# An attention and MLP kernel on one core: where the weights are converted, where GpSimd forms x0, and when pair 1 is loaded

## The chip, the cores and the metric

One core of a Trainium2 chip runs the whole kernel. The metric is the device time of one execution in microseconds (us). Engines: PE is TensorE (matmuls), DVE is VectorE, ACT is ScalarE, POOL is GpSimd, and SP is SyncE, which here only issues DMAs. Each engine runs its own queue in order.

## The reference

```
scores = q k^T / 8 + bias          # 4 batches, 8 heads, 576 x 576, head size 64
bias   = relu(psi(i,j) w1 + b1) w2 # a small MLP over positions, the same for all batches
attn   = exp(scores - max) / (sum + 1e-9)
x      = attn v                    # reshaped to 2304 tokens x 512
h      = x w_in                    # 512 -> 2048
out    = (h tanh(softplus(h))) w_out   # 2048 -> 512
```

`w_in` and `w_out` are float64 in DRAM; everything else is float32. The kernel splits each matmul operand into a high part (fp32r) and the remainder (low), and adds high x high, high x low and low x high.

## The kernel before

Three phases follow each other in one hand-ordered program (no planner reorders it; the order in which the Python issues instructions is the order of each engine's queue).

*Bias phase.* 36 groups (`idx` 0 to 35) of 16 positions each: `make_h` forms four `ht` tiles on ACT or DVE, PE multiplies them by w2 into `bps`, `evac` scales the result on ACT into one of eight `bt` buffers, and SP stores it to `bias_d` in DRAM. At the indices in `BIAS_AT` SP loads finished bias rows back for the first head pair. At `SOFT_AT` the first three attention steps are already issued. In between, `load_raw(1)` (SP: q/k rows and v of pair 1), `load_hi(1)` (a DMA from POOL's queue) and `load_weights` (SP: two weight tiles of 512 KB) are issued at fixed indices.

*Attention.* 16 pairs (a batch and two heads), 5 steps each, 80 steps (`NS`). A step does `scores` on PE, `add_bias` with the maximum on DVE, `exps` on ACT, `transposes` on PE and ACT of the step two before, and `pv_duo` on PE. For the next pair POOL subtracts the high from the full operand: `split_k` at a pair's second step, `split_q` at its third (for pair 1 both are issued at step 3). One MLP weight tile is converted over four steps: `high` (float64's upper word, scaled), `low` (a shift), two merging instructions on DVE (L125, L127), then ACT copies the high part and POOL subtracts the low part (L138). Half of the 32 tiles are done here. Near the end x of the first token block is loaded (`load_x`), with the reciprocals of the sums (`load_r`, two halves into one buffer), and POOL multiplies them (L375) at steps NS-8 and NS-4.

*MLP.* 72 units. A unit is one chunk of 128 hidden features for a block of 512 tokens (or two chunks for the block of 256). `hidden` is 12 matmuls, followed by Exp on ACT and two instructions on DVE (L600, L601). `gate`, one unit later, is Ln and Exp on ACT, two products on DVE (L611, L612), `ghi` on ACT and `glo = e - ghi` (L614, on POOL up to unit 23, then on DVE). `project`, three units later, is 12 matmuls. The first halves of blocks 0 and 1 (units 0 to 15) come first, then their second halves; `split_x(1)` prepares block 1 during units 2 to 7, and after block 0's first half its sums are copied out (L639). `convert` does the other 16 weight tiles: once before the loop's units, then behind the gate at units 3, 5, 7 and from 8 on at three of four units, with `high` on ACT and the subtraction on POOL.

The change touches `conv_weights` (L107 to L130), `ahead` and `split` (L358 to L391), the calls at L534 to L539 with `BIAS_AT` (L468), `gate` (L604) and the MLP loop (L698 to L743).

Of the kernel before, what the change touches and what calls it, by code (L numbers as in the profile page):

```python
# [7 lines left out]
F32 = mybir.dt.float32  # L8
F32R = mybir.dt.float32r
U32 = mybir.dt.uint32  # L10
AF = mybir.ActivationFunctionType
ALU = mybir.AluOpType
# [7 lines left out]
P = 128  # L20
# [26 lines left out]
def kernel(ctx: ExitStack, tc, qk, v, wb, w2, w_in, w_out, psia, psi4, rinv, eye, out):  # L47
# [18 lines left out]
    convp = sbuf("conv", 2)  # L66
# [19 lines left out]
    EARLY, HALF = 4, len(order) // 2  # L86
    ring = sbuf("ring").ring((HALF - EARLY) * 4096 + 2560)
    w_hi, w_lo = {}, {}
    todo, w64, w32 = list(order), [], []

    def alloc_weights(jobs, p):
        for job in jobs:
# [3 lines left out]
    def load_weights():  # L96
        while todo and len(w64) < 2:
            kind, g, k = job = todo.pop(0)
            w = convp.tile([P, 512, 2], U32, name="w64")
            if kind == "i":  # L100
                src = w_in[k * P:(k + 1) * P, g * 512:(g + 1) * 512]
            else:
                src = w_out[(4 * g + k) * P:(4 * g + k + 1) * P, :]
            sp.dma_start(out=w.rearrange("p f t -> p (f t)"), in_=src.bitcast(U32))
            w64.append((job, w))

    def conv_weights(on_act):  # L107

        job, w = w64.pop(0)
        c = convp.tile([P, 512], F32, name="w32")
        cu = c.bitcast(U32)
        high = convp.tile([P, 512], F32, name="high", bufs=1)
        low = convp.tile([P, 512], U32, name="low", bufs=1)
        hu = high.bitcast(U32)
        if on_act:
            act.mul(high, w.bitcast(F32)[:, :, 1], 2.0 ** -112)  # L118
        else:
            dve.tensor_scalar(high, w.bitcast(F32)[:, :, 1], 2.0 ** -112, None, op0=ALU.mult)  # L120

        def parts():
            dve.tensor_scalar(low, w[:, :, 0], 29, None, op0=ALU.logical_shift_right)
            yield False
            dve.scalar_tensor_tensor(cu, hu, 3, low, op0=ALU.logical_shift_left, op1=ALU.bitwise_or)  # L125
            yield False
            dve.scalar_tensor_tensor(cu, hu, 0x80000000, cu, op0=ALU.bitwise_and, op1=ALU.bitwise_or)  # L127
            w32.append((job, c))
            yield True
        return parts()  # L130

    def split_weights(eng):
        job, c = w32.pop(0)
        if job not in w_hi:
            w_hi[job] = ring.tile([P, 512], F32R, name="wh{}{}{}".format(*job))
            w_lo[job] = ring.tile([P, 512], F32R, name="wl{}{}{}".format(*job))
        act.copy(w_hi[job], c)
        eng.tensor_tensor(w_lo[job], c, w_hi[job].bitcast(F32), op=ALU.subtract)  # L138
# [188 lines left out]
            sp.dma_start(out=x_d[b][:, hp, 512:576], in_=x[:, 0:64])  # L327

    LAG = 2
    conv = []  # L330
    alloc_weights(order[:EARLY], wpool)

    x_raw, x_r, x_hi, x_lo = {}, {}, {}, {}
# [9 lines left out]
    def load_r(blk, r, h0, h1):  # L343

        t0, n = blocks[blk]
        for off, m, b, s in _x_runs(t0, n):
            while m:
# [7 lines left out]
                                 in_=src.unsqueeze(0).to_broadcast([64, h1 - h0, k]))  # L355
                off, m, s = off + k, m - k, s + k

    def ahead(n):  # L358

        i, x = divmod(n, 5)  # L360
        if x == 4 and i + 2 < NPAIR:
            load_hi(i + 2)
            load_raw(i + 2)
        if i % B == B - 1 and i // B + 1 < HP:
            load_bias(i // B + 1, ORDER[x])
        if n == NS - 11:
            load_x(0, x0)
        if n in (NS - 10, NS - 6):
            x_r[0] = x0.tile([P, 2, TB], F32, name="xr", bufs=1)
            h0 = 0 if n == NS - 10 else 2  # L370
            load_r(0, x_r[0], h0, h0 + 2)
        if n in (NS - 8, NS - 4):
            h0 = 0 if n == NS - 8 else 2
            for d in range(2):
                pool.tensor_tensor(x_raw[0][:, h0 + d], x_raw[0][:, h0 + d], x_r[0][:, d], op=ALU.mult)  # L375

    def split(n):

        i, x = divmod(n, 5)
        if (x == 1 or n == 3) and i + 1 < NPAIR:  # L380
            split_k(i + 1)
        if (x == 2 or n == 3) and i + 1 < NPAIR:
            split_q(i + 1)

        for _ in range((1, 1, 1, 1, 1)[x]):
            if not conv and w64[0][0] in order[:HALF]:
                conv.append(conv_weights(x == 2))
            elif conv and next(conv[0]):
                conv.clear()
                load_weights()  # L390
                split_weights(pool)  # L391

    def step(n):
        i, x = divmod(n, 5)
# [70 lines left out]
    spent = {"v": 0.0, "a": 0.0}  # L465
    maker = {}
    SOFT_AT = (18, 27, 35)
    BIAS_AT = (12, 20, 24, 32, 36)  # L468
    for idx, t in enumerate(ts):
        spent["a"] += 1.0 + (1.9 if idx in SOFT_AT else 0.0)  # L470
        spent["v"] += (1.7 if idx in SOFT_AT else 0.0) + (1.4 if idx in (9, 12) else 0.0)
# [37 lines left out]
    for idx in range(NB + 2):  # L509
        if idx < NB:  # L510
            t = ts[idx]
            make_h(idx + 2)
            n = reach(t)[2]
            ps = bps.tile([P, 1024], F32, name="bps")
            for a in range(0, n, 512):
                for cg in range(4):
                    pe.matmul(ps[cg * 32:cg * 32 + 32, a:min(a + 512, n)], w2t,  # L517
                              h_t[idx, cg][:, a:min(a + 512, n)], start=True, stop=True)
            bps_t[t] = ps
        if 1 <= idx <= NB:  # L520
            evac(ts[idx - 1])
        if idx == 1:
            load_raw(0)
        if idx == 9:
            split_k(0)
        if idx == 12:
            split_q(0)
        if idx in BIAS_AT:
            load_bias(0, ORDER[BIAS_AT.index(idx)])
        for lag, do in enumerate((scores, add_bias, exps)):  # L530
            if idx - lag in SOFT_AT:
                for u in range(2 if lag == 2 else 1):
                    do(SOFT_AT.index(idx - lag), *((u,) if lag == 2 else ()))
        if idx == 14:  # L534
            load_raw(1)
        if idx == 18:
            load_hi(1)
        if idx == 26:
            load_weights()  # L539
    bias_scope.close()  # L540

# [16 lines left out]
    def split_x(blk, parts):  # L558
        n = blocks[blk][1]
        if blk not in x_hi:  # L560
            x_hi[blk] = xp.tile([P, HP, TB], F32R, name="xhi")
            x_lo[blk] = xp.tile([P, HP, TB], F32R, name="xlo")
        for x, d in parts:
            raw, hi, lo = (y[blk][:, d, :n] for y in (x_raw, x_hi, x_lo))
            if x == "h":
                if blk:

                    dve.tensor_tensor(raw, raw, lo.bitcast(F32), op=ALU.mult)
                act.copy(hi, raw)  # L569
            else:  # L570
                dve.tensor_tensor(lo, raw, hi.bitcast(F32), op=ALU.subtract)  # L571
# [29 lines left out]
        dve.scalar_tensor_tensor(e, e, 2.0, e, op0=ALU.add, op1=ALU.mult)  # L601
        h_t[blk, fs] = (h, e)

    def gate(blk, fs, eng=dve):  # L604
        r = mp.tile([P, TB], F32, name="r")
        ghi = mp.tile([P, TB], F32R, name="ghi")
        glo = mp.tile([P, TB], F32R, name="glo")
        h, e = h_t.pop((blk, fs))
        act.activation(r, e, AF.Ln, bias=two[:, 0:1])
        act.activation(r, r, AF.Exp, scale=-1.0)  # L610
        dve.tensor_tensor(e, h, e, op=ALU.mult)  # L611
        dve.tensor_tensor(e, e, r, op=ALU.mult)  # L612
        act.copy(ghi, e)  # L613
        eng.tensor_tensor(glo, e, ghi.bitcast(F32), op=ALU.subtract)  # L614
        gs[blk, fs] = (ghi, glo)

    def stage(name):
# [77 lines left out]
    wq = sbuf("wq")  # L695
    y_ps = psum("y_ps", 1)
    alloc_weights(order[HALF:], wq)
    done = []  # L698

    def convert():  # L700

        if done:
            split_weights(done.pop())
        if w64:
            for _ in conv_weights(True):
                pass
            load_weights()
            done.append(pool)

    gate(*units[0], pool)  # L710
    hidden(*units[1])
    convert()
    gate(*units[1], pool)
    hidden(*units[2])

    for k in range(2, len(units) + LAG2):
        if k < len(units):
            blk, fs = units[k]
            f = fs[0]
            if k < FH:  # L720
                split_x(1, XPARTS[:2] if k == 2 else XPARTS[2:4] if k == 3 else XPARTS[k:k + 1])
            elif blk == 1 and f == FH:
                fetch_x(2)
            elif blk == 0:
                if f == FH:
                    fetch_r(2)
                if f == FH + 5:
                    load_kept()
                if f >= FH + 3:
                    split_x(2, {3: XPARTS[:2], 4: XPARTS[2:4]}.get(f - FH, XPARTS[f - FH - 1:f - FH + (f == NFC - 1)]))  # L730
            elif 2 <= blk < len(blocks) - 1:
                if f == 2:
                    fetch(blk + 1)
                if f >= 8:
                    split_x(blk + 1, XPARTS[f - 8:f - 8 + len(fs)])
            if k > 2:
                hidden(blk, fs)
        if k >= LAG2:
            project(*units[k - LAG2])
        if 2 <= k - 1 < len(units):  # L740
            gate(*units[k - 1], pool if k < 3 * FH else dve)
        if k > 2 and (k % 4 < 3 if k >= FH else k % 2):
            convert()  # L743


# [55 lines left out]
```

## Time and profile before

| | us |
|---|---|
| median of 3 runs | 753.96 (752.93 to 755.56) |
| the profiled execution | 754.99 |
| its span in the profile | 752.1 |

| engine | busy us in the span |
|---|---|
| PE | 712.2 |
| DVE | 514.3 |
| ACT | 467.9 |
| POOL | 181.8 |

In the trace the bias phase and the first steps fill the time to about 66 us, attention lasts to about 328, and the MLP the rest. Matmuls are pipelined, so a busy PE is not a PE at full rate: compare how much work passes in a stretch. A row of a timeline has the start, the us of the whole entry and its instruction; the brackets hold the idle time before it and what ended that. A row of busy time by stretch has the stretch and its length, the busy us and instructions of PE, PEld, DVE, ACT and POOL, PE's granted clock (1.00 is full), the DMA engines' share and GB/s. A row of groups by line has the count, busy us, mean ns, and the idle time before.

### The profile page before, as it was taken

What the parts mean: (1) busy time and instruction counts of PE and PEld (TensorE: products, weight loads), DVE (VectorE), ACT (ScalarE), POOL (GpSimd) and SP (SyncE); (2) the same over time, 40 slices, a digit from 0 to 9 for tenths busy, and PEclk for the clock granted to TensorE, in tenths of its full rate; (3) what the DMA queues carried; (4) which work ended last, traced back from release to release, by engine and by line L of the source; (5) the groups of instructions that cost most, each with busy time, mean ns of one, the idle gap of its engine ahead of it and who ended that gap; (6) DMA issues with size and microseconds to landing.
All of it is one profiled execution on the core that took longest, in us unless ns stands there. A gap on an engine that the chain in (4) does not pass through costs nothing.

```text
span 752.1 us, 11589 instructions
## 1 busy us (share of the span) xinstructions
PE 712.2 (95%) x4144; PEld 544.4 (72%) x4144; DVE 514.3 (68%) x987; ACT 467.9 (62%) x995; POOL 181.8 (24%) x113
## 2 busy tenths in 40 slices
PE   6769999999999999899989999999999999999997
PEld 2226777777777777658767776688998888888886
DVE  7995767768677764346877777777576666665554
ACT  6877877887888787665455455555454554444443
POOL 1110443565444453402343433300100000000000
PEclk9979999999999999999998999999999999999999
DMA  8987759648866977141113311132304000010001
GB/s 276 308 256 249 242 165 298 214 161 276 258 205 186 299 242 222 45 128 37 57 56 112 112 57 56 29 113 79 90 1 120 22 0 1 1 56 1 1 0 57
DMA packets 46681, 95.68 MB, mean 127 GB/s; under 512 B 13456, under 2 KB 22304, under 8 KB 44576
## 3 DMA queue, kind: packets, MB, share of 16 engines
q1 hardware_dynamic: 43744, 74.80, 32.9%
q0 software_dynamic: 2304, 19.92, 7.8%
q8 instruction: 32, 0.52, 0.3%
q10 hardware_dynamic: 576, 0.22, 0.1%
q14 instruction: 25, 0.20, 0.1%
HBM read 73.48 MB, written 21.45 MB: 126 GB/s over the span
## 4 chain that ended last, share of the span: by engine, by line
PE 66%; DVE 17%; ACT 8%; issue 4%; DMA 2%; POOL 2%; SPq 1%; DVEq 0%; ACTq 0%; POOLq 0%
PE y L632 18%; PE h L594 17%; PE s L220 11%; PE o L315 8%; PE tp L282 6%; DVE w L127 3%; PE bps L517 3%; DVE w L125 2%; DVE e L601 2%; DVE e L612 2%; DVE e L600 2%; PE o L319 2%; DVE e L611 2%; DMA xr<-r_d 2%; ACT high L118 1%
## 5 line engine op out<-in xcount | busy, mean ns | idle before, releaser
L251 ACT ACTIVATE pt<-pt,m 128x576 f32<-128x576 f32 x144 | 112.7, 784 | 53.0 <-DVE m L236 52.4
L236 DVE CUSTOM_DVE_ANT_0 pt<-s,bias 128x576 f32<-128x576 f32 x144 | 103.7, 752 | 55.3 <-PE s L220 53.5
L613 ACT CAST ghi<-e 128x512 fp32r<-128x512 f32 x72 | 44.7, 621 | 143.7 <-DVE e L612 139.7
L632 PE MATMUL y<-who,glo 128*128 128x512 f32 x288 | 114.4, 397 | 5.9 <-POOL glo L614 5.9
L632 PE MATMUL y<-who,ghi 128*128 128x512 f32 x288 | 114.1, 396 | 4.4 <-ACT xraw L639 2.2
L632 PE MATMUL y<-wlo,ghi 128*128 128x512 f32 x288 | 113.2, 393 | 0.0
L594 PE MATMUL h<-xhi,whi 128*128 128x512 f32 (+1 forms) x320 | 80.3, 372 | 1.0 <-ACT xhi L569 0.9
L594 PE MATMUL h<-xlo,whi 128*128 128x512 f32 (+1 forms) x320 | 79.0, 368 | 0.0
L594 PE MATMUL h<-xhi,wli 128*128 128x512 f32 (+1 forms) x320 | 78.8, 368 | 0.0
L220 PE MATMUL s<-qkhi 128*128 128x288 f32 x320 | 77.1, 322 | 0.7 <-issue 0.4
L315 PE MATMUL o<-main,vt 128*64 128x320 f32 (+1 forms) x512 | 75.8, 418 | 1.2 <-DVE x L322 1.2
L600 DVE TENSOR_SCALAR e<-e 128x512 f32<-128x512 f32 x72 | 36.5, 507 | 57.5 <-ACT e L599 57.5
L220 PEld LDWEIGHTS s<-qkhi 128*128 128x128 f32 x320 | 49.5, 189 | 34.1 <-issue 28.6
L220 PE MATMUL s<-qkhi,qlo 128*128 128x288 f32 x320 | 69.1, 297 | 3.6 <-POOL qlo L182 3.6
L177 POOL TENSOR_TENSOR qkhi<-rawqk,qkhi 64x1216 fp32r<-64x1216 f32 x15 | 42.7, 2844 | 118.5 <-DMA rawqk<-in_qk_dram 55.2
L632 PEld LDWEIGHTS y<-who,glo 128*128 128x128 f32 x288 | 54.6, 190 | 22.1 <-POOL glo L614 10.9
L599 ACT ACTIVATE e<-h 128x512 f32<-128x512 f32 x72 | 42.6, 591 | 43.5 <-PE h L594 43.5
L283 ACT COPY main<-tp 128x512 f32<-128x512 f32 x128 | 68.0, 581 | 0.7 <-PE tp L282 0.2
L632 PEld LDWEIGHTS y<-who,ghi 128*128 128x128 f32 x288 | 54.5, 189 | 19.0 <-ACT ghi L613 4.2
L282 PE MATMUL tp<-ident,pt 128*128 128x128 f32 x512 | 67.4, 275 | 0.7 <-ACT main L283 0.7
L594 PEld LDWEIGHTS h<-xhi,whi 128*128 128x128 f32 x320 | 57.8, 190 | 13.5 <-ACT xhi L569 2.4
L594 PEld LDWEIGHTS h<-xlo,whi 128*128 128x128 f32 x320 | 56.9, 189 | 10.4 <-DVE xlo L571 0.4
(75 smaller groups left out, 1210.6 us busy)
## 6 DMA issues: line engine op xcount, KB each, us to landing
qkhi<-in_qk_dram POOLq DMA_DIRECT2D x16, 1216.0 KB, 8.7
bias_d<-bt SPq DMA_DIRECT2D x36, 295.5 KB
rawqk<-in_qk_dram SPq DMA_DIRECT2D x32, 304.0 KB
w<-in_w_in_dram SPq DMA_DIRECT2D x16, 512.0 KB
w<-in_w_out_dram SPq DMA_DIRECT2D x16, 512.0 KB
vt<-in_v_dram SPq DMA_DIRECT2D x16, 320.0 KB
bias<-bias_d SPq DMA_DIRECT2D x16, 288.0 KB
out_dram<-w SPq DMA_DIRECT2D x17, 256.0 KB
```

Source lines behind the costliest of these rows:

```text
L177: (pool if i else dve).tensor_tensor(kl, qk_raw[i][64:128], kl.bitcast(F32), op=ALU.subtract)
L220: pe.matmul(s[:, j, :SH], stat[:, q0:q0 + P], hi[:, QW + kc + j * SH:QW + kc + (j + 1) * SH], start=(k == 0), stop=(k == len(todo) - 1))
L236: dve.tensor_tensor_reduce(out=halves(pt[:, sl]), in0=s[:, :, :SH], in1=halves(bt[:, sl]), scale=-0.125, scalar=BIG, op0=ALU.add, op1=ALU. ...
L251: act.activation(ps, ps, AF.Exp, bias=m[:, u:u + 1], scale=-1.0, accum_out=sums[i][:, k:k + 1])
L282: pe.transpose(tp[:, k * P:(k + 1) * P], pt[:, c0:c0 + P], ident)
L283: act.copy(main[:, h, :, off:off + P], tp.rearrange("p (k q) -> p k q", k=4))
L315: pe.matmul(o[h * 64:h * 64 + 64, :w], vt[:, h, k, :], main[:, h, k, :], start=(k == 0), stop=False, **kw)
L594: pe.matmul(h[:, u * n:(u + 1) * n], w["i", g4, d][:, r * P:(r + 1) * P], x[:, d, :n], start=(k == 0), stop=(k == 11))
L599: act.activation(e, h, AF.Exp)
L600: dve.tensor_scalar(e, e, E20, None, op0=ALU.min)
L613: act.copy(ghi, e)
L632: pe.matmul(ys[blk][t], g[:, c0:c0 + P], w, start=((blk, f) in first and k == 0), stop=((blk, f) in last and k == 2))
```

## The change

The conversion is cut into four functions with a list `half` between them: `scale_high`, `shift_low` (which also loads the next weight tile), `merge` and `sign`. In attention they keep one part per step. In the MLP a loop over all units issues, at units 0, 2, 4, 6, 7 and from 8 on at two of three, `scale_high` on ACT at the head of the unit; the other three parts stand on DVE between `ghi` and `glo` of the same unit, and `split_weights` at the head of the next, with its subtraction on DVE. `glo` is always on DVE. `split_x(1)` is spread over units 0 to 6. POOL's x0 products move one step later (NS-7 and NS-3). `load_raw(1)`, `load_hi(1)` and `load_weights` move to indices 32, 33 and 36 of the bias phase, and two entries of `BIAS_AT` change.

```diff
     todo, w64, half, w32 = list(order), [], [], []
-    def conv_weights(on_act):
+    def scale_high(eng):
         job, w = w64.pop(0)
-        c = convp.tile([P, 512], F32, name="w32")
         high = convp.tile([P, 512], F32, name="high", bufs=1)
-        low = convp.tile([P, 512], U32, name="low", bufs=1)
-        if on_act:
+        if eng is act:
             act.mul(high, w.bitcast(F32)[:, :, 1], 2.0 ** -112)
         else:
             dve.tensor_scalar(high, w.bitcast(F32)[:, :, 1], 2.0 ** -112, None, op0=ALU.mult)
+        half.append((job, w, high))
+
+    def shift_low():
+        job, w, high = half.pop(0)
+        low = convp.tile([P, 512], U32, name="low", bufs=1)
+        dve.tensor_scalar(low, w[:, :, 0], 29, None, op0=ALU.logical_shift_right)
+        half.append((job, high, low))
+        load_weights()
+
+    def merge():
+        job, high, low = half.pop(0)
+        c = convp.tile([P, 512], F32, name="w32")
+        dve.scalar_tensor_tensor(c.bitcast(U32), high.bitcast(U32), 3, low, ...)
+        half.append((job, high, c))
+
+    def sign():
+        job, high, c = half.pop(0)
+        cu = c.bitcast(U32)
+        dve.scalar_tensor_tensor(cu, high.bitcast(U32), 0x80000000, cu, ...)
+        w32.append((job, c))
...
     def ahead(n):
-        if n in (NS - 8, NS - 4):
-            h0 = 0 if n == NS - 8 else 2
+        if n in (NS - 7, NS - 3):
+            h0 = 0 if n == NS - 7 else 2
             for d in range(2):
                 pool.tensor_tensor(x_raw[0][:, h0 + d], x_raw[0][:, h0 + d], x_r[0][:, d], op=ALU.mult)
...
     def split(n):
-            if not conv and w64[0][0] in order[:HALF]:
-                conv.append(conv_weights(x == 2))
-            elif conv and next(conv[0]):
-                conv.clear()
-                load_weights()
-                split_weights(pool)
+        if half:
+            parts.pop(0)()
+        elif w64[0][0] in order[:HALF]:
+            scale_high(act if x == 2 else dve)
+            parts.extend((shift_low, merge, lambda: (sign(), split_weights(pool))))
...
-    BIAS_AT = (12, 20, 24, 32, 36)
+    BIAS_AT = (12, 20, 24, 30, 37)
...
-        if idx == 14:
+        if idx == 32:
             load_raw(1)
-        if idx == 18:
+        if idx == 33:
             load_hi(1)
-        if idx == 26:
+        if idx == NB:
             load_weights()
...
-    def gate(blk, fs, eng=dve):
+    def convert():
+        shift_low()
+        merge()
+        sign()
+
+    def gate(blk, fs):
...
         act.copy(ghi, e)
-        eng.tensor_tensor(glo, e, ghi.bitcast(F32), op=ALU.subtract)
+        if half:
+            convert()
+        dve.tensor_tensor(glo, e, ghi.bitcast(F32), op=ALU.subtract)
...
-    def convert():
-        if done:
-            split_weights(done.pop())
-        if w64:
-            for _ in conv_weights(True):
-                pass
-            load_weights()
-            done.append(pool)
-    gate(*units[0], pool)
-    hidden(*units[1])
-    convert()
-    gate(*units[1], pool)
-    hidden(*units[2])
-    for k in range(2, len(units) + LAG2):
+    SHARE = {0: XPARTS[0:1], 1: XPARTS[1:2], 2: XPARTS[2:4], 3: XPARTS[4:5], 4: XPARTS[5:6], 5: XPARTS[6:7], 6: XPARTS[7:]}
+
+    for k in range(len(units) + LAG2):
+        on = k % 3 < 2 if k >= FH else k in (0, 2, 4, 6, 7)
+        if w32:
+            split_weights(dve)
+        if on and w64:
+            scale_high(act)
         if k < len(units):
...
             if k < FH:
-                split_x(1, XPARTS[:2] if k == 2 else XPARTS[2:4] if k == 3 else XPARTS[k:k + 1])
+                split_x(1, SHARE.get(k, ()))
...
-            if k > 2:
+            if k > 0:
                 hidden(blk, fs)
         if k >= LAG2:
             project(*units[k - LAG2])
-        if 2 <= k - 1 < len(units):
-            gate(*units[k - 1], pool if k < 3 * FH else dve)
-        if k > 2 and (k % 4 < 3 if k >= FH else k % 2):
+        if 0 <= k - 1 < len(units):
+            gate(*units[k - 1])
+        elif half:
             convert()
```

## Rows read from the trace of the kernel before

**Rows 1.** The page's first part: busy us (share of the span) xinstructions

```profile
PE 712.2 (95%) x4144; PEld 544.4 (72%) x4144; DVE 514.3 (68%) x987; ACT 467.9 (62%) x995; POOL 181.8 (24%) x113
```

**Rows 2.** Chain of waits, steady MLP: start us, us, what xcount

```profile
498.92 2.72 PE h L594 x12
501.64 2.72 PE y L632 x12
```

**Rows 3.** PE in order of time, then busy time by stretch of the MLP

```profile
348.74 1.07 PE L594 MATMUL h<-xhi,whi 128*128 128x512 f32 x4
...
348.74:498.92 150.18, 139.84 (x578) 108.36 (x577) 112.97 (x157) 77.65 (x135) 53.87 (x37) 0.98 0.20 66
498.92:737.00 238.08, 238.08 (x1142) 201.00 (x1141) 151.68 (x250) 116.29 (x193) 2.59 (x2) 1.00 0.12 34
```

**Rows 4.** DVE's wait for high (total, times, longest); DVE, POOL timelines of conversions

```profile
DVE w L125 <- ACT high L118: 23.2, 15, 1.6
...
452.87 0.78 DVE L125 SCALAR_TENSOR_TENSOR w<-high,low 128x512 uint32<-128x512 uint32 x1 [1.55 <-ACT high L118]
453.69 1.67 DVE L127 SCALAR_TENSOR_TENSOR w<-high,w 128x512 uint32<-128x512 uint32 x1
...
388.07 1.75 POOL L138 TENSOR_TENSOR wli<-w,whi 128x512 fp32r<-128x512 f32 x1
```

**Rows 5.** DVE timeline at 342; DVE's groups by line, 498.92 to 737

```profile
342.65 0.42 DVE L123 TENSOR_SCALAR low<-w 128x512 uint32<-128x512 uint32 x1
...
343.90 0.69 DVE L127 SCALAR_TENSOR_TENSOR w<-high,w 128x512 uint32<-128x512 uint32 x1
...
L614 DVE TENSOR_TENSOR glo<-e,ghi 128x512 fp32r<-128x512 f32 x45 | 31.2, 692 | 33.2 <-ACT ghi L613 33.2
L612 DVE TENSOR_TENSOR e<-e,r 128x512 f32<-128x512 f32 x44 | 30.5, 693 | 4.6
...
L600 DVE TENSOR_SCALAR e<-e 128x512 f32<-128x512 f32 x44 | 18.7, 426 | 43.4 <-ACT e L599 43.4
```

**Rows 6.** PE timeline where block 0's sums are copied out

```profile
395.63 0.50 PE L632 MATMUL y<-who,ghi 128*128 128x512 f32 x1 [2.18 <-ACT xraw L639]
```

**Rows 7.** Chain of waits; PE timeline; POOL timeline, attention's last pairs

```profile
264.48 1.26 PE s L220 x8
...
281.06 1.26 PE s L220 x8
...
318.92 1.26 PE s L220 x8
...
307.43 0.85 PE L220 MATMUL s<-qkhi,qlo 128*128 128x288 f32 x2 [2.92 <-POOL qlo L182]
...
295.60 2.77 POOL L177 TENSOR_TENSOR qkhi<-rawqk,qkhi 64x1216 fp32r<-64x1216 f32 x1 [8.95 <-DMA rawqk<-in_qk_dram]
302.17 2.51 POOL L375 TENSOR_TENSOR xraw<-xraw,xr 128x512 f32<-128x512 f32 x2 [3.79 <-DMA xr<-r_d]
```

**Rows 8.** Bias phase: POOL and DVE timelines, line L490, DMA by stretch, SP

```profile
2.85 1.24 POOL L172 DMA_DIRECT2D qkhi<-in_qk_dram  x2
...
35.39 2.78 POOL L177 TENSOR_TENSOR qkhi<-rawqk,qkhi 64x1216 fp32r<-64x1216 f32 x1 [31.30 <-DMA rawqk<-in_qk_dram]
...
35.57 5.60 DVE L490 TENSOR_SCALAR ht<-at,bb 128x304 f32<-128x304 f32 x2
...
L490 DVE TENSOR_SCALAR ht<-at,bb x120: 359/446/2890, 5.1 to 58.1; 128x544 f32<-128x544 f32 x8, 128x352 f32<-128x352 f32 x8, 128x320 f32<-128x320 f32 x8, 128x496 f32<-128x496 f32 x7
...
60.00:66.00 6.00, 5.21 (x38) 3.83 (x39) 2.64 (x7) 4.66 (x11) 0.00 (x0) 1.00 0.95 314
66.00:68.00 2.00, 1.92 (x16) 1.32 (x16) 0.00 (x0) 1.93 (x6) 0.00 (x0) 1.00 0.04 17
...
67.04 0.33 SPq L191 DMA_DIRECT2D bias<-bias_d  x1
...
70.67 0.76 DVE L236 CUSTOM_DVE_ANT_0 pt<-s,bias 128x576 f32<-128x576 f32 x1 [0.23 <-PE s L220]
```

More of the change, by code (lines that the diff above doesn't have):

```diff
@@ L88 @@
     w_hi, w_lo = {}, {}
-    todo, w64, w32 = list(order), [], []
+    todo, w64, half, w32 = list(order), [], [], []
     def alloc_weights(jobs, p):
@@ L105, in load_weights @@
             w64.append((job, w))
-    def conv_weights(on_act):
+    def scale_high(eng):
         job, w = w64.pop(0)
-        c = convp.tile([P, 512], F32, name="w32")
-        cu = c.bitcast(U32)
         high = convp.tile([P, 512], F32, name="high", bufs=1)
-        low = convp.tile([P, 512], U32, name="low", bufs=1)
-        hu = high.bitcast(U32)
-        if on_act:
+        if eng is act:
             act.mul(high, w.bitcast(F32)[:, :, 1], 2.0 ** -112)
@@ L120, in conv_weights @@
             dve.tensor_scalar(high, w.bitcast(F32)[:, :, 1], 2.0 ** -112, None, op0=ALU.mult)
[L122 to L130, printed above, removed]
+        half.append((job, w, high))
[8 more added lines that the diff above has]
+        c = convp.tile([P, 512], F32, name="w32")
+        dve.scalar_tensor_tensor(c.bitcast(U32), high.bitcast(U32), 3, low,
+                                 op0=ALU.logical_shift_left, op1=ALU.bitwise_or)
+        half.append((job, high, c))
+    def sign():
+        job, high, c = half.pop(0)
+        cu = c.bitcast(U32)
+        dve.scalar_tensor_tensor(cu, high.bitcast(U32), 0x80000000, cu,
+                                 op0=ALU.bitwise_and, op1=ALU.bitwise_or)
+        w32.append((job, c))
     def split_weights(eng):
@@ L329 @@
     LAG = 2
-    conv = []
     alloc_weights(order[:EARLY], wpool)
@@ L356, in load_r @@
                 off, m, s = off + k, m - k, s + k
+    parts = []
     def ahead(n):
@@ L383, in split @@
             split_q(i + 1)
-        for _ in range((1, 1, 1, 1, 1)[x]):
-            if not conv and w64[0][0] in order[:HALF]:
-                conv.append(conv_weights(x == 2))
-            elif conv and next(conv[0]):
-                conv.clear()
-                load_weights()
-                split_weights(pool)
+        if half:
[3 more added lines that the diff above has]
+            parts.extend((shift_low, merge, lambda: (sign(), split_weights(pool))))
     def step(n):
@@ L697 @@
     alloc_weights(order[HALF:], wq)
-    done = []
-    def convert():
-        if done:
-            split_weights(done.pop())
-        if w64:
-            for _ in conv_weights(True):
-                pass
-            load_weights()
-            done.append(pool)
-    gate(*units[0], pool)
-    hidden(*units[1])
-    convert()
-    gate(*units[1], pool)
-    hidden(*units[2])
-    for k in range(2, len(units) + LAG2):
+    SHARE = {0: XPARTS[0:1], 1: XPARTS[1:2], 2: XPARTS[2:4], 3: XPARTS[4:5], 4: XPARTS[5:6], 5: XPARTS[6:7], 6: XPARTS[7:]}
[5 more added lines that the diff above has]
+            scale_high(act)
         if k < len(units):
```

## The prediction

> **What bounds the kernel now.** I read first the page's busy list, then the chain of waits, then each stage by itself. TensorE (PE) is busy for 95% of the span [rows 1], but its busy time is pipelined, so I compare rates instead. In the MLP one unit is 12 matmuls of `hidden` and 12 of `project`, in the steady part 2.72 + 2.72 = 5.44 us [rows 2]. Between the fifth `hidden` at 348.74 and the 29th at 498.92 lie 24 units in 150.18 us [rows 2, 3], 6.26 us each. At the steady rate they would take 24 x 5.44 = 130.6, so **19.6 us** are lost there; from 498.92 on PE runs without a gap, and its busy time in that stretch is the whole stretch [rows 3].
>
> In the 150 us VectorE (DVE) sets the pace. Each of the 15 conversions in it waits for ScalarE's `high` (23.2 us in all) [rows 4], because `high` stands in ScalarE's queue behind `ghi` and the weight copy, which wait for DVE's own gate products. Then the last part of the conversion takes 1.67 [rows 4], against 0.69 for the same instruction at 343.90 [rows 5]; beside it GpSimd runs `glo` and then the weight subtraction of 1.75 [rows 4]. PE also loses 2.18 at 395.63 waiting for the copies of block 0's kept half [rows 6].
>
> In attention a pair takes 16.58 (264.48 to 281.06); the two periods to 318.92 take 37.86 instead of 33.16, so **4.70** are lost in one place [rows 7]. PE stands 2.92 before `qlo`, up to 307.43, and the slower matmuls after the stop make up the other 1.8. `qlo` stood on GpSimd behind two x0 products, which started at 302.17 after 3.79 of waiting for the r_d load [rows 7].
>
> In the bias phase DVE loses time to GpSimd: the split of pair 1 starts at 35.39, when its raw load has landed, and two DVE `ht` instructions, which take 0.36 at the shortest, take 5.60 together beside it [rows 8]. That is **4.9** lost on an engine that is then busy without a pause.
>
> **The change, part by part.**
>
> *MLP conversion.* `high` goes to the head of ScalarE's iteration, before that iteration's `exp`, so the 23.2 of waiting go: by the time DVE comes to it, `high` was issued a whole unit earlier. GpSimd gets no `glo` and no weight subtraction here any more; DVE gets both, at 0.69 each (the form of `glo`, 128x512, 45 times in the steady part) [rows 5]; the weight subtraction has not run on DVE, and its nearest row is this one. DVE per unit: `e` 0.43 once, 0.69 three times (one of the three alike rows stands), `glo` 0.69: 3.19. A converting unit adds 0.42 (342.65), twice 0.69 (343.90, and a row like it before it; GpSimd was idle there) and 0.69 for the weight subtraction: 2.49, so 5.68 [rows 5]. Two units in three convert from unit 8 on, and the third still waits 33.2 / 45 = 0.74 for `ghi` [rows 5], which in converting units the conversion covers. Mean: (2 x 5.68 + 3.19 + 0.74) / 3 = 5.10, under PE's 5.44. So PE becomes the bound again, with only 6% to spare, and the gain is at most 19.6.
>
> What the new order costs: `glo` now stands behind the conversion on DVE, and PE's `project` waits for `glo`. The slack is three units, so this costs nothing where DVE keeps up. It does not in the first eight units: 8 x 3.19 + 5 conversions x 2.49 + 8 instructions for block 1's x (0.69) = 43.5, against 8 x 5.44 = 43.5 for PE, with nothing left for hand-overs. Following the queues by hand from the end of attention (DVE in the order sub, x, `e`, `e`, product, product, conversion, `glo`), unit 1's `glo` ends about 2.7 us after PE wants it. With the ratio of the x0 stop (2.92 cost 4.70) that is 4.3; I take 4.0, from 1 (the stop at 395.63 goes in exchange) to 9 (the stop comes at two units). MLP: 19.6 - 4.0 = **15.6** (10 to 19).
>
> The trace shows 0.69 and 1.67 for one instruction, the long one where GpSimd works [rows 4, 5]. The Trainium skill, SBUF — State Buffer, "Who interferes with whom", says that a VectorE instruction with two SBUF inputs and a GpSimd one that reads SBUF take an exclusive lock, so the later is blocked in full. By that rule, with no GpSimd work beside it, the price is 0.69; were 0.78 and 1.67 the price in this place, the mean would be 5.81. The trace agrees with the rule, since 0.69 and 1.67 stand within one stage.
>
> *x0 products behind the last split.* On GpSimd `qlo` would run right after the K split, which starts at 295.60 and takes 2.77 [rows 7]; with as much again for `qlo` it is ready at 301.2, before 304.5, where PE stops. The products still start when r_d has landed, 302.17, since nothing of that load moves; the second load waits for them as before, and x0 is split only after the last scores, over 14 us later [rows 7]. So nothing new is late: 4.70 at most. Nothing would be gained if PE stopped for something else at 304.5. I take **4.5** (2 to 4.7).
>
> *Loads at the end of the bias phase.* Moving `load_hi(1)` is worth nothing: GpSimd issues it at 2.85 together with `load_hi(0)` [rows 8], since nothing stands before it in that queue, and this stays so. Moving `load_raw(1)` from behind the 14th of the 36 bias stores to behind the 32nd takes GpSimd's split out of the phase: DVE wins up to 4.9. ScalarE and the stores must follow. The DMA engines carry 314 GB/s at 60 to 66 [rows 8]. The weights (2 x 512 KB) move behind the last store, 3.3 us at that rate, ahead of the last bias load, which SP issued at 67.04, after the engines had stood nearly idle from 66 to 68 [rows 8]; its reader starts at 70.67 and waits only for PE [rows 8]. The weights fill the 2 idle us, so that load may come 1.3 later against the stores. And GpSimd's split of pair 1 now ends some 5.6 behind the raw load's landing (twice the 2.78 at 35.39), near to where pair 1's scores want it; DVE's first `high` must pass it and the weights. Also SP waits for bias rows earlier (index 30). Ends: +4.9, and -4.3 (no gain, 1.3 for the weights, 3.0 for 0.93 MB of raw data before the last stores). I take **3.0**: the 4.9 less 1.9 for these two.
>
> *Conversion in attention.* The four parts stand at the same steps; the next weight is loaded two steps earlier, behind loads that SP has already issued. 0, with 1 us either way: attention is set by PE's 16.58 per pair [rows 7].
>
> **Sum.** 15.6 + 4.5 + 3.0 = 23.1. The profiled execution took 754.99 (span 752.1, 2.9 around it); 754.99 - 23.1 = 731.9. It lay 1.0 above the median 753.96, so against the median I forecast **731**.
>
> **The rivals.**
>
> *A: DVE stays the bound, at long conversions.* If 0.78 and 1.67 are their price (DVE slowed by something other than GpSimd), a converting unit takes 3.19 + 0.42 + 0.78 + 1.67 + 0.69 = 6.75, the mean is 5.81, and 24 units gain 24 x (6.26 - 5.81) = 10.8; with 7.5 from the other two places 754 - 18.3 = 736. For it: 1.67 in nearly every MLP conversion. Against it: the 0.69 at 343.90.
>
> *B: the hand-overs eat the MLP gain.* A converting unit at 6.67 instead of 5.68 ((2 x 6.67 + 5.44) / 3 = 6.26): no gain there, 754 - 7.5 = 746.5. It takes 1.0 more per unit, as much as `e` waits for ScalarE in the steady part (43.4 / 44 = 0.99) [rows 5]. For it: six hand-overs a unit between DVE and ScalarE in fixed order. Against it: in the steady part that wait is PE's slack, not a bound.
>
> *C, slower: all hand-overs in a row.* `glo` is queued behind the conversion and the next weight subtraction behind `glo`; if `e`'s 0.99, `ghi`'s 0.74 [rows 5] and a wait like `high`'s 1.55 [rows 4] for the weight copy all fall between DVE's instructions, a converting unit takes 5.68 + 3.28 = 8.96, the mean 7.79, and 24 units 187: 37 more, 783 at worst with the 7.5 gained. With the first two alone it is 7.41, mean 6.75, 162, and 754 + 11.8 - 7.5 = **758**. It is slower than before from 7.14 per converting unit on. Against it: those waits exist only where DVE is early, and here it would be late.
>
> *D: nothing moves,* because what ends each wait is replaced at once (a load for the x0 products, the bias stores, PE's start of the MLP): 754. The 19.6 speak against it, since PE has no other bound in that stretch than DVE.
>
> **How the numbers follow.** Forecast 0.66, its own range 723 to 742; A 0.13; B 0.10; C 0.07; D 0.04. The range 722 to 746 holds the forecast's extremes (19 + 4.7 + 4.9 = 28.6 gained gives 725; with a little for the unknown attention part 722), A, and half of B; C, D and the other half of B are some 0.16. A measurement of this kernel tells a difference from about 0.3% (2.3 us): faster 0.66 + 0.13 + 0.10 = 0.89, within 0.3% 0.04, slower 0.07.
>
> **What would show it.** In the profile after: no wait of the conversion for `high` in the MLP and its last part at about 0.69; 24 units from the fifth `hidden` in 131 to 136, most of the rest lost in units 1 to 3 in front of `glo`; no stop of PE before `qlo` at the last pair, and a steady 16.58; no `ht` of 2.8 in the bias phase, whose end (DVE's reader of the last bias, now at 70.67) lies 2 to 5 earlier; GpSimd's `load_hi(1)` at 3 as before. The prediction is wrong if PE still waits for `glo` at every converting unit, or if the bias phase ends later than now, behind the weights.

## The result and the profile after

The kernel after takes **737.23 us** (median of 4 runs, 736.07 to 738.0) against 754.06 for the kernel before (4 runs, 752.93 to 755.56): ratio 0.9774, interval 0.9752 to 0.9797, or 16.8 us less. The forecast was 731, 23 less; the time lies 6 above it, inside its range. The profiled execution took 736.07 (span 733.9), 18.9 less than the one before; the stretches below are of these two.

The page's first part, which answers to [rows 1]:

```profile
PE 702.2 (96%) x4144; PEld 542.5 (74%) x4144; DVE 506.6 (69%) x1026; ACT 469.7 (64%) x995; POOL 125.5 (17%) x74
```

POOL has 39 instructions fewer, DVE 39 more. The chain of waits of after (start us, us, what), which answers to [rows 2, 7]:

```profile
57.01 7.65 DMA bias_d<-bt
...
265.84 1.26 PE s L228 x8
...
282.42 1.25 PE s L228 x8
...
299.00 1.25 PE s L228 x8
...
315.58 1.25 PE s L228 x8
...
502.91 2.87 PE h L600 x24
```

Attention's steady 16.58 now holds to the end: 265.84 to 315.58 is three times it. The first row, a bias store on the chain, is the subject of the bias phase below. The row with x24 is the first block of 256 tokens. Its place in the chain of before, and rows of before's timelines that are needed to compare (PE: the second group of transposes, the first `pv_duo` and the first `hidden`; DVE: the third soft step's `add_bias` and the first copy of x):

```profile
520.68 2.87 PE h L594 x24
```

```profile
65.38 1.14 PE L282 MATMUL tp<-ident,pt 128*128 128x128 f32 x8 [0.46 <-ACT main L283]
...
67.53 1.95 PE L315 MATMUL o<-main,vt 128*64 128x256 f32 x16
...
328.40 2.06 PE L594 MATMUL h<-xhi,whi 128*128 128x512 f32 x4 [0.94 <-ACT xhi L569]
```

```profile
62.32 0.76 DVE L236 CUSTOM_DVE_ANT_0 pt<-s,bias 128x576 f32<-128x576 f32 x1 [3.70 <-PE s L220]
...
70.02 0.42 DVE L322 COPY x<-o 128x256 f32<-128x256 f32 x1 [4.94 <-PE o L319]
```

The same places on PE of after:

```profile
65.39 1.15 PE L290 MATMUL tp<-ident,pt 128*128 128x128 f32 x8 [3.96 <-ACT main L291]
...
68.20 2.79 PE L323 MATMUL o<-main,vt 128*64 128x256 f32 x16
...
325.05 2.06 PE L600 MATMUL h<-xhi,whi 128*128 128x512 f32 x4 [0.93 <-ACT xhi L575]
...
347.00 1.07 PE L600 MATMUL h<-xhi,whi 128*128 128x512 f32 x4
...
351.96 0.50 PE L645 MATMUL y<-who,glo 128*128 128x512 f32 x1 [1.01 <-DVE glo L627]
```

From these rows the account by stage (us of the profiled executions; a plus is time gained):

| stretch | before | after | gained | forecast |
|---|---|---|---|---|
| start to the first copy of x | 70.02 | 71.53 | -1.5 | +3.0 |
| from there to the chain's row at 264.48 / 265.84 | 194.46 | 194.31 | +0.2 | 0 |
| from there to 318.92 / 315.58 (x0 products) | 54.44 | 49.74 | +4.7 | +4.5 |
| from there to the first `hidden` | 9.48 | 9.47 | 0 | 0 |
| first `hidden` to the first 256-token block | 192.28 | 177.86 | +14.4 | +15.6 |
| the rest of the span | 231.42 | 230.99 | +0.4 | 0 |
| outside the span | 2.9 | 2.2 | +0.7 | 0 |
| sum | | | +18.9 | +23.1 |

**The bias phase** is where the forecast failed. DVE in order of time, then ACT, SP and the busy time by stretch:

```profile
35.71 10.30 DVE L496 TENSOR_SCALAR ht<-at,bb 128x304 f32<-128x304 f32 x32
45.93 0.74 DVE L244 CUSTOM_DVE_ANT_0 pt<-s,bias 128x576 f32<-128x576 f32 x1
...
58.83 0.76 DVE L244 CUSTOM_DVE_ANT_0 pt<-s,bias 128x576 f32<-128x576 f32 x1 [5.03 <-PE s L228]
...
71.53 0.43 DVE L330 COPY x<-o 128x256 f32<-128x256 f32 x1 [3.24 <-PE o L327]
72.19 0.76 DVE L244 CUSTOM_DVE_ANT_0 pt<-s,bias 128x576 f32<-128x576 f32 x1 [0.24 <-PE s L228]
```

```profile
64.75 1.07 ACT L291 COPY main<-tp 128x512 f32<-128x512 f32 x2 [3.49 <-DMA bias_d<-bt]
```

```profile
54.64 0.60 SPq L171 DMA_DIRECT2D rawqk<-in_qk_dram  x1
...
57.01 3.46 SPq L509 DMA_DIRECT2D bias_d<-bt  x4
60.52 1.69 SPq L104 DMA_DIRECT2D w<-in_w_in_dram  x2
66.62 0.33 SPq L199 DMA_DIRECT2D bias<-bias_d  x1
```

```profile
66.00:68.00 2.00, 1.92 (x12) 1.51 (x11) 0.30 (x1) 1.91 (x6) 2.00 (x1) 0.63 0.67 224
68.00:70.00 2.00, 2.00 (x12) 1.05 (x12) 0.29 (x1) 0.87 (x5) 0.00 (x0) 0.51 0.80 288
```

Read it in that order. 32 `ht` instructions take 10.30, with none of 2.8 among them as in [rows 8], and the third soft step's `add_bias` starts at 58.83 (62.32 before): DVE's gain arrived, 3.5 of it. Then ACT's first copy into `main` waits 3.49 for a DMA with which its data have nothing to do, a bias store. The reading is that `main` lies in memory that `bt` used; e2 and e5 below test it. The last four stores were issued from 57.01 on, behind the raw load of 54.64, and SP's wait for them ends at 66.62. So PE's second transposes start at 65.39, where they started at 65.38 before: all 3.5 are gone. And after the 3.96 in which PE stood, the granted clock is 0.63 and 0.51 of full up to 70 (0.5 is the lower of the two levels, 1.2 of 2.4 GHz); the first `pv_duo` takes 2.79 (1.95 before), and x comes 1.5 later than before.

**GpSimd and the MLP** did as forecast. GpSimd issues `load_hi(1)` at 2.85, as before; `qlo` runs ahead of the x0 products. POOL in order of time, DVE inside one converting unit, and 24 units by stretch:

```profile
299.95 2.79 POOL L190 TENSOR_TENSOR qlo<-rawqk,qkhi 64x1216 fp32r<-64x1216 f32 x1
302.69 2.54 POOL L384 TENSOR_TENSOR xraw<-xraw,xr 128x512 f32<-128x512 f32 x2
```

```profile
377.44 0.69 DVE L129 SCALAR_TENSOR_TENSOR w<-high,low 128x512 uint32<-128x512 uint32 x1
378.16 0.69 DVE L136 SCALAR_TENSOR_TENSOR w<-high,w 128x512 uint32<-128x512 uint32 x1
378.77 0.68 DVE L627 TENSOR_TENSOR glo<-e,ghi 128x512 fp32r<-128x512 f32 x1
379.54 0.69 DVE L146 TENSOR_TENSOR wlo<-w,who 128x512 fp32r<-128x512 f32 x1
```

```profile
347.00:481.15 134.15, 131.91 (x578) 107.95 (x577) 116.66 (x195) 77.74 (x133) 0.00 (x0) 1.00 0.23 75
```

No wait for `high` stands before L129, and the last part takes 0.69 where [rows 4] have 1.67. The 24 units take 134.15 instead of 150.18 [rows 3]; from 391 on PE runs at 2.72 per 12 matmuls. All PE waits from 340 to 500 us end by 391.07, the first of them (1.1, for `ghi`) before the stretch of the 24 units begins (waits: total, times, longest):

```profile
PE y L645 <- ACT ghi L624: 1.4, 2, 1.1
...
PE y L645 <- DVE glo L627: 1.0, 1, 1.0
...
PE y L645 <- ACT xraw L652: 0.8, 1, 0.8
```

### The profile page after: what moved, and what is told of

The parts are those of the page before. It is cut to its first block, busy times and chain, and to the rows that moved or that the text cites. A ratio compares the mean times of both kernels' runs of the same rounds, so it can differ in the third digit from the quotient of the medians.

```text
span 733.9 us, 11563 instructions
## 1 busy us (share of the span) xinstructions
PE 702.2 (96%) x4144; PEld 542.5 (74%) x4144; DVE 506.6 (69%) x1026; ACT 469.7 (64%) x995; POOL 125.5 (17%) x74
## 4 chain that ended last, share of the span: by engine, by line
PE 76%; DVE 7%; ACT 4%; DMA 2%; issue 1%; SPq 1%; POOL 1%; DVEq 0%; ACTq 0%
PE y L645 24%; PE h L600 23%; PE s L228 11%; PE o L323 8%; PE tp L290 6%; PE o L327 2%; DMA w<-in_w_in_dram 1%; DMA bias_d<-bt 1%; DVE w L136 1%; PE tp L303 1%; DVE e L623 1%; DVE e L607 1%; PE tp L293 1%; DVE e L622 1%; ACT main L291 1%
## 5 line engine op out<-in xcount | busy, mean ns | idle before, releaser
L645 PE MATMUL y<-who,ghi 128*128 128x512 f32 x288 | 112.5, 391 | 2.2 <-ACT ghi L624 1.4
L645 PE MATMUL y<-who,glo 128*128 128x512 f32 x288 | 112.4, 390 | 1.1 <-DVE glo L627 1.0
L627 DVE TENSOR_TENSOR glo<-e,ghi 128x512 fp32r<-128x512 f32 x72 | 49.8, 691 | 42.0 <-ACT ghi L624 42.0
L606 DVE TENSOR_SCALAR e<-e 128x512 f32<-128x512 f32 x72 | 30.6, 426 | 54.5 <-ACT e L605 54.5
```

The costliest lines, as they stand in the source:

```text
L627: dve.tensor_tensor(glo, e, ghi.bitcast(F32), op=ALU.subtract)
L645: pe.matmul(ys[blk][t], g[:, c0:c0 + P], w, start=((blk, f) in first and k == 0), stop=((blk, f) in last and k == 2))
```

## The experiments

The theory after this reading: (a) the bias term was lost because the last stores stand behind the raw load in SP's queue and `main` waits for a store through shared memory; (b) the whole MLP gain needs both edits, `high` first and GpSimd out. Rivals: the store wait is only what shows, and the weights or last bias load would end the phase just as late; or the MLP gain comes from one of the two edits alone. Medians were taken with the kernel before on the same chip at 754.1 to 754.4.

**e1: the raw load back at index 14.**

```diff
-        if idx == 32:
+        if idx == 14:
```

> The changed kernel with load_raw(1) alone moved back to index 14. Theory (the raw load's 0.93 MB stood ahead of the last four bias stores, and ACT's first copy into main has to wait until those stores have landed, because main lies in the memory of bt): the two long ht come back (5.60 for two near 35 to 41), DVE ends its ht about 4.9 later, but ACT's copy into main no longer waits 3.5 for bias_d, and DVE's first x copy (71.53 in the changed kernel, 70.02 in the one before) comes at 70.0 to 70.8; in all 0.7 to 1.5 us less than the changed kernel. Rival (the weights' load behind the last store, or the later last bias load, sets the end): the first x copy stays at 71.5 or comes later, up to 75, and the whole is 0 to 4 us more.

735.29 (735.03 to 736.58), ratio 0.9769 (0.9718 to 0.982). The wait of `main` is gone and DVE's stop beside GpSimd (split at 36.25 to 41.9) is back; two of PE's waits of 40 to 80 us:

```profile
PE bps L523 <- DVE ht L496: 2.5, 2, 1.7
PE tp L290 <- ACT main L291: 0.5, 2, 0.3
```

First copy of x at 70.46, 1.1 before that of after. So one wait was exchanged for another. By the medians the move of this load costs 1 to 2, but after's own copy of x differs by more than that from profile to profile (see after again, below), so e1 gives no price.

**e2: the pool of `main` opened after the two pools of x,** to take it off the stores' memory.

```diff
+    x0 = lsbuf("x0")
+    xs = lsbuf("xs", 2)
     ptp = lsbuf("ptp", 1)
-    xs = lsbuf("xs", 2)
-    x0 = lsbuf("x0")
```

> The changed kernel with three pools opened in another order, so that main lies over bt buffers whose stores were issued before the raw load. Theory (the wait is one for memory): PE's stop of 3.96 before its transposes at 61 goes to under 1, its granted clock stays up at 66 to 70, and the next thing late is the last bias load (issued 66.6, landing near 70); DVE's reader of it comes at 69.5 to 71 instead of 72.2; gain 1.2 to 2.7 us. Rival (ACT waits for the DMA engines in general, or PE for something else): the stop stays near 4, no gain.

739.27 (738.76 to 740.02), 0.9817 (0.9774 to 0.986): slower, a miss. ACT's wait:

```profile
ACT main L291 <- DMA bias_d<-bt: 4.6, 1, 4.6
```

The copy starts at 65.89, just after SP's last bias load, which needs every store, could start (65.83): the new place seems to cover `bt` buffers of still later stores. The expectation was wrong on where the memory lies. That the wait grows by 1.1 when only the memory moves agrees with shared memory as its cause; one profile does not show it (e5 does).

**e3: the raw load at index 29,** three stores earlier (the expectation's eight is a miscount), ahead of the stores that `main` needs.

```diff
-        if idx == 32:
+        if idx == 29:
```

> The changed kernel with load_raw(1) at index 29: after DVE has nearly all of its ht behind it, but ahead of the wait for index 30's bias rows and eight stores earlier. Theory (order in SP's queue): the last four stores land about 3 earlier, near 62 instead of 64.7 to 66.6, PE's stop before main shrinks from 3.96 to 1 or less, the last bias load is issued at 62 to 64; GpSimd's split of pair 1 runs at 54 to 60, where DVE has no ht left, so no ht of 2.8 returns; DVE's first x copy at 67.5 to 69 instead of 71.53; gain 2.5 to 4 us. Rival (the stage is bound by the bytes of all DMAs, so the place does not matter): x copy at 71 or later, gain under 0.7.

**732.91** (731.76 to 734.97), 0.9735 (0.969 to 0.978): 4.3 less than after in the medians. `main` waits 1.2, the last bias load is issued at 63.18 (66.62), and DVE's copy of x comes 5.2 earlier, more than expected:

```profile
66.34 0.42 DVE L330 COPY x<-o 128x256 f32<-128x256 f32 x1 [1.63 <-PE o L327]
```

DVE stays undisturbed, since the split runs at 54.67. Against before that is +3.7 in this stretch: the forecast's 3.0 was to be had, with the load three stores earlier. The rival (something else ends the phase as late) falls. Not all of the 5.2 reaches the end: the profiled execution is only 2.5 shorter than that of after. Attention gives back 1.1, and the stretch from the first `hidden` to the 256-token block takes 179.38 instead of 177.86, since PE's granted clock falls at its start, to 0.61 in the mean:

```profile
322.00:326.00 4.00, 3.98 (x10) 2.94 (x11) 1.41 (x3) 0.44 (x1) 0.00 (x0) 0.61 1.00 263
```

**e4: the x0 products back** at their old steps.

```diff
-        if n in (NS - 7, NS - 3):
+        if n in (NS - 8, NS - 4):
```

> The changed kernel with GpSimd's x0 products back at steps NS-8 and NS-4, ahead of the last q split. Theory (queue order on GpSimd): PE's stop of about 2.9 before qlo returns near 304, the slower clock after it too, and the whole is 4.2 to 4.9 us more than the changed kernel. Rival (another cover ends the wait there, as the load of pair 15's own rows): 0 to 1.5 us more.

738.34 (736.45 to 740.86), 0.9806 (0.9758 to 0.9854): 1.1 more than after in the medians, not 4.2 to 4.9. The time is the rival's (0 to 1.5 more), its mechanism is not: PE still waits for `qlo`. The chain of waits, then PE:

```profile
283.05 1.26 PE s L228 x8
...
317.76 1.26 PE s L228 x8
```

```profile
307.77 0.53 PE L228 MATMUL s<-qkhi,qlo 128*128 128x288 f32 x2 [1.29 <-POOL qlo L190]
```

r_d lands where it did (GpSimd's products start at 302.48, 302.17 before), PE comes 2.0 later (306.48, 304.51 before), so the stop is 1.29 instead of 2.92 [rows 7] and no slow matmuls follow it. The two periods take 34.71, 1.6 over 33.16, where before lost 4.70. So with PE's new timing this edit is worth 1.6 here; the rest of the 4.7 had gone with PE's later arrival.

**m1: `glo` of units 0 to 23 and the weight subtraction back on GpSimd,** `high` still first.

```diff
-        dve.tensor_tensor(glo, e, ghi.bitcast(F32), op=ALU.subtract)
+        (pool if len(gs_n) < 24 else dve).tensor_tensor(glo, e, ghi.bitcast(F32), op=ALU.subtract)
+        gs_n.append(1)
...
-            split_weights(dve)
+            split_weights(pool)
```

> The changed kernel with glo (units 0 to 23) and the weight subtraction back on GpSimd; high stays at the head of ScalarE's unit. Theory (DVE is kept waiting by GpSimd while both read SBUF): the last conversion instruction takes 1.3 to 1.7 again instead of 0.69 in most units, DVE has less work but no less time, and from hidden of unit 0 to the first hidden of the 256-token block 183 to 192 us pass instead of 177.9: 5 to 14 us more in all. Rival (1.67 was not GpSimd's doing; DVE is relieved of 0.69 to 1.38 per unit): 175 to 178 us, the same or up to 3 us less.

754.02 (749.64 to 757.04, 10 runs), 0.9989 (0.9963 to 1.0015): the whole gain is gone. First `hidden` to the 256-token block takes 195.36, worse than expected and than before (192.28). DVE's waits of 340 to 500 us, then DVE, POOL and ACT in order of time:

```profile
DVE e L606 <- ACT e L605: 35.5, 25, 1.8
```

```profile
406.41 0.69 DVE L129 SCALAR_TENSOR_TENSOR w<-high,low 128x512 uint32<-128x512 uint32 x1
407.14 1.66 DVE L136 SCALAR_TENSOR_TENSOR w<-high,w 128x512 uint32<-128x512 uint32 x1
```

```profile
406.88 1.37 POOL L627 TENSOR_TENSOR glo<-e,ghi 128x512 fp32r<-128x512 f32 x1 [3.25 <-issue]
```

```profile
408.83 0.62 ACT L145 CAST whi<-w 128x512 fp32r<-128x512 f32 x1 [2.08 <-DVE w L136]
409.36 0.66 ACT L114 ACTIVATE high<-w 128x512 f32<-128x512 f32 x1
409.92 0.58 ACT L605 ACTIVATE e<-h 128x512 f32<-128x512 f32 x1
```

No wait for `high` is left, and yet nothing is gained: L136 is long again beside GpSimd (1.65 or 1.66 in all 15 conversions of 340 to 500 us), the weight copy on ACT waits for it, and the next unit's exp stands behind that copy. DVE then waits for exp at each of 25 units, 1.42 on average. That is rivals B and C's mechanism, hand-overs in a row; GpSimd's presence sets it off.

**m2: `high` where the conversion begins,** GpSimd still out: behind `ghi` in ACT's queue, as before the change.

```diff
         act.copy(ghi, e)
-        if half:
+        if on_now[0] and w64:
+            scale_high(act)
             convert()
...
+        on_now[0] = on
...
-        if on and w64:
-            scale_high(act)
         if k < len(units):
```

> The changed kernel with high issued where the conversion begins, behind ghi, as in the kernel before; glo and the weight subtraction stay on DVE. Theory (the place of high on ScalarE matters by itself): DVE waits 0.7 to 1.0 for high in each of 16 conversions, which lifts its mean per three units over PE's 5.44, and the same stretch takes 181 to 187 us instead of 177.9: 3 to 9 more. Rival (freeing DVE of GpSimd was the whole gain, and the wait is hidden by the slack): 178 to 179.

744.72 (742.87 to 745.0), 0.9865 (0.9832 to 0.9899). The stretch takes 186.40, inside the 181 to 187 expected. DVE's waits of 340 to 500 us:

```profile
DVE w L129 <- ACT high L114: 14.4, 15, 1.0
```

With before and after this is a table of two by two (the stretch in us). The cell of before is not a clean one: there the conversion also stands behind `glo` and at other units.

| | `glo`, subtraction on GpSimd | on DVE |
|---|---|---|
| `high` behind `ghi` | 192.28 (before) | 186.40 (m2) |
| `high` first | 195.36 (m1) | 177.86 (after) |

From after, taking back `high` costs 8.5 and taking back GpSimd 17.5, each by a change of that one thing. Against before, GpSimd out alone gives 5.9, `high` first alone -3.1, both together 14.4. So neither edit alone gives the whole gain, and theory (b) holds. What the other changes of this stretch give by themselves (the conversion ahead of `glo`, two units of three instead of three of four, block 1's x over units 0 to 6) was not tested.

**m3: the first conversion before the last `pv_duo`** of attention, so that one fewer falls in units 0 to 7.

```diff
     hidden(*units[0])
+    scale_high(act)
     step(NS + 1)
+    convert()
...
-        on = k % 3 < 2 if k >= FH else k in (0, 2, 4, 6, 7)
+        on = k % 3 < 2 if k >= FH else k in (2, 4, 6, 7)
```

> The changed kernel with the first MLP conversion taken out of unit 0 and put ahead of the last attention products, where DVE stood idle for 3.1 us (331.4 to 334.5). Theory (the first eight units are bound by DVE, which has as much work as PE there): the stretch shrinks by 1.0 to 2.4 us and so does the whole. Rival (PE's stops in units 1 to 3 come from the hand-overs between DVE and ScalarE, whatever DVE's load): 0 to 0.5.

735.51 (735.02 to 736.82), 0.9754 (0.9716 to 0.9792). The stretch takes 175.96, 1.9 less than in after. That is clear of chance: in the six profiles with after's MLP code, e3 left aside, it takes 177.83 to 177.87, and in b1 and b2, which have this edit too, 176.00. So part of the start's residue is DVE's work in the first eight units, as the forecast put it; the rival's 0 to 0.5 falls.

**b1: e3 and m3 together.**

> Both changes that promise a gain together: load_raw(1) at index 29 and the first conversion in DVE's idle time. Theory: they lie 260 us apart and add up, 729.5 to 732.5. Rival (what is won early is lost again where the MLP starts, at a load or at PE's granted clock): 732.5 to 734.

732.53 (729.29 to 734.04), 0.9703 (0.9664 to 0.9742); profiled 729.29. The median lies on the border of theory and rival: by the medians m3's part does not show beyond e3's, and the four runs are too far apart to settle it. In the profile the first 256-token block is at 495.92, 7.0 earlier than in after, and the clock at the MLP's start stays at 1.00; in e3 the rival's drop of the clock did occur.

**e5: `main` of the second head group in a pool of its own,** ordered so that the first lies clear of all stores; the raw load as in after.

```diff
+    x0 = lsbuf("x0")
+    xs = lsbuf("xs", 2)
+    ptp1 = lsbuf("ptp1", 1)
     ptp = lsbuf("ptp", 1)
-    xs = lsbuf("xs", 2)
-    x0 = lsbuf("x0")
...
-            main = ptp.tile([P, 2, 4, w], F32, name=f"main{grp}")
+            main = (ptp1 if grp else ptp).tile([P, 2, 4, w], F32, name=f"main{grp}")
...
```

> The changed kernel with the first group's main and tail put behind all other tiles, where no bt buffer lay; the second group's main takes the place over bt. Theory (ACT's copy into main waits for bias stores only because main lies over bt): the wait of 3.5 before the first copy into main goes to 0, PE's stop before its transposes at 61 to under 0.7 and its granted clock stays full there; the second group's first copy waits for the last stores instead, until about 66; then the last bias load (landing near 70) sets the pace; DVE's first x copy at 67 to 70.5 instead of 71.5, 1 to 3 us less in all. Rival (the wait is for something else that ends at the same time): the stop stays near 4 and the time too.

737.1 (732.87 to 738.97), 0.9755 (0.9709 to 0.9802): no change. PE, then DVE:

```profile
60.54 1.15 PE L290 MATMUL tp<-ident,pt 128*128 128x128 f32 x8 [0.36 <-ACT main L291]
...
71.76 0.82 PE L228 MATMUL s<-qkhi 128*128 128x288 f32 x2 [5.42 <-issue]
```

```profile
70.90 0.76 DVE L244 CUSTOM_DVE_ANT_0 pt<-s,bias 128x576 f32<-128x576 f32 x1 [2.53 <-DMA bias<-bias_d]
```

The stop of 3.96 is gone: the cause of that wait is shown. The second group's first copy, whose tile now lies over `bt`, waits 3.35 for a bias store instead, until 66.59, and the copy of x comes at 67.95, both as expected. But the last bias load still waits for the last stores (issued at 66.54), `add_bias` and PE now stop for it, and the granted clock falls to 0.57 and 0.50 at 70 to 74: the first `hidden` is at 328.30, 3.3 later than in after. The wait was passed on to the next reader. Taking one reader off the late stores is not enough; the stores have to be earlier.

**b2: all three (e3, m3, e5),** beside **the kernel after once more.**

> All three that promise a gain: load_raw(1) at index 29, main clear of bt, the first conversion in DVE's idle time. Theory: with the load at 29 the wait for bt is only 0.3 to 1.2, so main's place adds 0 to 1 to what the other two give: 728.5 to 732.5. Rival (the last bias load or the weights' load then set the end of the phase): no difference from the two alone, 732 to 733.

> The changed kernel itself once more, on the chip and among the runs of the two others, so that they are compared with it and not only with the kernel before: 736 to 738 by every theory; ACT's wait before main between 1 and 4.6 as in the other runs with this bias phase, and the time 2 to 4 us less where it is under 2.

b2: **729.59** (728.16 to 730.95, 6 runs), 0.9673 (0.9645 to 0.9702); after again: 736.5 (733.87 to 737.74, 6 runs), 0.9761 (0.973 to 0.9792). b2 beats both kernels, by 6.9 and by 24.5. In b2 no stop of PE from 55 to 80 us is over 0.71, and the copy of x is at 65.79. In the profile of after again the wait of `main` is 2.4, the copy of x at 68.75, and the granted clock stays at 1.00 from 60 us on; PE there:

```profile
64.10 1.15 PE L290 MATMUL tp<-ident,pt 128*128 128x128 f32 x8 [2.88 <-ACT main L291]
```

So the bias term is not one number. In the six profiles with the same code in this phase (after, after again, e4, m1, m2, m3) the wait of `main` is 1.06 to 3.51 and the copy of x at 67.36 to 71.53, 2.7 earlier to 1.5 later than in the one profile of before, 0.3 earlier in the mean. At its best it comes near the forecast's 3.0; the -1.5 of the account is its worst. With the load at index 29 (e3, b1, b2) the copy is at 65.79 to 66.34, earlier than in any of the six.

## Why the prediction was right or wrong

- *MLP: right, over by 1.2.* 24 units were forecast at 131 to 136 and took 134.15; the mechanism held in each part (no wait for `high`, 0.69, PE the bound again, the loss at the start). The mis-sized term is the residue: 19.6 - 14.4 = 5.2 instead of 4.0, made of 1.6 before the fifth `hidden` (347.00 - 325.05 = 21.95, against 348.74 - 328.40 = 20.34) and 3.6 in the 24 units (134.15 - 130.6).
- *Rival A is out,* though its 736 lies nearer to the measured 737 than the forecast's 731 does: in the MLP every conversion is short without GpSimd (0.69) and long with it (1.66 in m1). *B and C* did not happen here, but m1 shows that their mechanism is real and takes the whole gain; the forecast gave them 0.17 on an argument, and had not seen that GpSimd is what decides.
- *x0: the number right, the cause in part.* 4.7 for 4.5, no stop before `qlo`, and "nothing new is late" held. What the forecast missed is that the place is worth this only while PE arrives early: with PE 2.0 later (e4) the old place costs 1.6. So the terms of the sum are not independent: some 3.1 of the 4.7 would have gone by PE's lateness alone, and that much of the agreement is luck.
- *Attention conversion: right,* 0.2 for 0.
- *The step that failed: "Loads at the end of the bias phase ... I take 3.0: the 4.9 less 1.9".* It measured -1.5 in the profile, and +0.3 in the mean of the six. By the prediction's own sign (the bias phase ends later than now, behind the weights) the first half came true, DVE's reader at 72.19 instead of 70.67, but behind the stores. The 4.9 was right on DVE (4.8 by its second soft step, 45.93 against 50.74), and 3.5 of it reached the third. Wrong was what the text set against it: it priced the load's traffic (1.3 for the weights and 3.0 for the raw data, of which it took 1.9 without a working) and looked for who reads the last *bias load*. It did not ask who waits for the last *stores*. There were two: that load, and `main`, whose memory `bt` had held. Measured by its own parts, the term is +3.5 (DVE's gain), -3.5 (PE's second transposes no earlier than before, for the stores) and -1.5 (slow matmuls after the stop); the second is near the 3.0 for raw data, most of which the forecast had left out of its sum. e3 and b2 show that the step's price is of order and not of traffic: the same bytes three stores earlier give +3.7 and +4.2 (b2 with `main` moved as well).
- *The whole:* the profiled executions differ by 18.9, 4.2 less than 23.1: 4.5 less from this step, 1.2 less from the MLP, and some 1.5 more from x0 and the terms put at 0. The medians differ by 16.8, since the profiled execution of after was the shortest of its four runs.

## What to carry to other kernels

Before a load is moved in a queue, list what stands behind it there, and for each store among that, everyone who waits for its end: the readers of what it writes, and the tiles that take over the memory it reads from. Two edits of one pipeline are to be priced together: the hand-over that one removes can come back through the other's, as `high` first did beside GpSimd. When a wait is removed, look for the next reader of the same late transfer before counting the gain.

## What the runs showed of the hardware that was not expected

- *The price of a stop is not its length.* A stop of PE of 2.92 before `qlo` was followed by slow matmuls [rows 7] (granted clock 0.50 at 308 to 310), one of 2.88 in after again by none (1.00 from 64 to 70), one of 3.96 by 0.63 and 0.51 for 4 us, one of 1.29 (e4) by none. The stop of 0.93 or 0.94 before the first `hidden` is in every profile; in e3 alone the clock fell after it (0.73 and 0.50 from 322 to 326), in the other twelve it stayed at 1.00. What decides is not shown.
- *Who starts first pays less, in m1.* There L129 began at 406.41, ahead of GpSimd's `glo` at 406.88, and kept its 0.69, while `glo` took 1.37 (mostly 1.28 in units without a conversion); L136 began at 407.14, behind it, and took 1.66, up to 0.55 after `glo`'s end. That agrees with the Trainium skill, SBUF — State Buffer, "Who interferes with whom": the order of issue decides who is blocked.
- *A store behind the raw load lands late, wherever that load stands.* The profile tells the landing of some stores only. Behind the load (2 x 304 and 320 KB) a store took 7.9 us from issue to landing in after, 7.0 in after again and 6.2 in m1, where others, ahead of the load, took 3.9 to 4.9. With the load at index 29 (e3, b2) one behind it took 6.7; with the load at index 14 (e1) one issued at 32 to 36 took 7.6, and the last ones, from 60 on, 3.5. By the Trainium skill, DMA: Bandwidth & Descriptors, "Two DMAs through the same engine are not ordered", descriptors within one queue of one DMA engine start in order, though they need not finish so. The trace agrees with the first part: the late store moves with the load.
